# One chunk of an input load cut into transfers of 112, 8 and 8 partitions, in a fused cross-covariance attention and StarReLU kernel

## The chip, the cores and the metric

The kernel runs on one core of a Trainium2 chip. The metric is the device time of one execution in microseconds. Before the change it is 718.32 us, the median of four runs (718.17 to 718.49).

## The reference

For each of 4 batches, `q`, `k` and `v` are 6080 x 256 arrays in float32. The attention is taken between the 256 channels, not between the tokens, and its result goes through a small two-layer network:

```python
qn = q / (np.linalg.norm(q, axis=1, keepdims=True) + 1e-06)    # norms over the 6080 tokens
kn = k / (np.linalg.norm(k, axis=1, keepdims=True) + 1e-06)
s = kn.transpose(0, 2, 1) @ qn / tau                           # 256 x 256 per batch
s = s - s.max(-1, keepdims=True)
a = np.exp(s); a /= a.sum(-1, keepdims=True) + 1e-09
x = (v @ a).reshape(24320, 256)
h = x @ w_in                                                   # 256 x 2048
r = np.maximum(h, 0.0)
out = (s_moe * (r * r) + b_moe) @ w_out                        # 2048 x 256
```

## The kernel before

**Start.** Nothing of the network can run until the channel matrix of batch 0 is known, and that needs every row of `q` and `k` of batch 0: 6080 rows of 256 floats each, 12.5 MB in all. The rows are cut into 13 chunks (`make_chunks`): eleven of 512 rows (128 partitions, four rows in each), one of 256 rows (128 partitions, two rows each) and one of 192 rows (96 partitions, two rows each). Below, k4 is the `k` part of chunk 4, the fifth chunk, q4 its `q` part, and so on.

Chunks 0 and 1 are loaded as float32 by the queues of SyncE and ScalarE and cast on VectorE and ScalarE. All later ones are loaded by GpSimd's queue, which turns float32 into float16 on the way. `Gram.load` (line 118) issues one transfer for the `k` part and one for the `q` part of a chunk (line 132): 512 KB read and 256 KB written for a chunk of 512 rows. GpSimd's program order is k2, q2, k3, q3, ... k9, q9, then k10, k11, k12, q10, q11, q12, then the first tile of `v`, five pieces of `w_in`, a second tile of `v`, four pieces of `w_out`, and so on.

Eight semaphores are used in turn by GpSimd's transfers. A transfer has to wait until the one eight places ahead of it, which has the same semaphore, has landed. So at most eight of GpSimd's transfers are in flight. A chunk's tile comes from `qk_pool`, which has eight buffers; chunk 12 takes the buffer of chunk 4.

**Use of a chunk.** For each chunk TensorE adds `q`-transposed times `k` into the 256 x 256 matrix `s_ps` (`Gram.mm`, line 148). ScalarE and VectorE square both arrays, and VectorE folds the squares (`norm_ops`, lines 171 to 221), for the norms. `keep_busy` (line 477) puts idle matmuls after chunks 5 to 9. After the last chunk come the norms (lines 244 and 248), their inverse (line 269), the exponential (line 300), and the product of the channel matrix with `w_in` into `wa` (lines 327 and 343).

**The rest.** From then on TensorE works through 48 groups of 512 tokens: `h` from `wa` and the transposed `v` (line 658), and the second layer (lines 730 and 826). The Gram matrices of batches 1 to 3 are computed between these steps; their chunks are loaded by the same function. The order on every engine is the program's.

Of the kernel before, what the change touches and what calls it, by code (L numbers as in the profile page):

```python
# [17 lines left out]
def kernel(  # L18
# [12 lines left out]
    nc = tc.nc  # L31
    P = 128
# [23 lines left out]
    def po(ins):  # L56

        tc.keep_in_program_order(ins)
        return ins
# [51 lines left out]
    class Gram:  # L111
# [7 lines left out]
        def load(self, c, parts=(0, 1)):  # L119

            at, np_, jc = self.chunks[c]
            if 0 in parts:
                self.raw[c] = qk_pool.tile([P, 2, JC, C], FP16, tag="qk", name="qk")
            t = self.raw[c]
            direct = self.b == 0 and c < NDIRECT
            for i in parts:
                src = (k, q)[i]
                rows = src[self.b, at : at + np_ * jc, :].rearrange("(p j) c -> p j c", j=jc)
                if direct:
                    (nc.sync, nc.scalar)[i].dma_start(out=raw32[:, c, i], in_=rows)  # L130
                else:
                    po(nc.gpsimd.dma_start(out=t[:np_, i, :jc, :], in_=rows))
            self.tiles[c] = t[:, 1], t[:, 0]

        def cast(self, c):
# [437 lines left out]
    for i, f in enumerate(folds):  # L573
        early.setdefault(FOLDS[i], []).append(f)
    at_step(14, lambda: po(nc.vector.tensor_scalar_mul(
        out=s_out, in0=s_bc, scalar1=1.0 / (LAM * LAM))))
# [343 lines left out]
```

## Time and profile before

| | |
|---|---|
| median of four runs | 718.32 us |
| the profiled execution | 718.25 us, of which the span from the first to the last instruction is 716.5 us and 1.75 us lie around it |
| mean granted TensorE clock | 0.997 |
| TensorE busy (matmul) | 697.0 us, 97% |
| VectorE, ScalarE, GpSimd busy | 624.2, 545.0 and 111.1 us |
| GpSimd's transfers (q0) | 43.40 MB, 38.1% of the 16 DMA engines' span |
| read from and written to HBM | 78.91 MB and 24.90 MB |

All times in the views are microseconds from the start of the span. In the chain of waits, each line has a start, a length, and what the end of the kernel was waiting for in that time. In a timeline, the bracket at the end of a line has the idle time of the engine ahead of the instruction and what ended it. A transfer is shown on the engine that issues it, with the time for the issue; its landing is later.

### The profile page before, as it was taken

What the parts mean: (1) busy time and instruction counts of PE and PEld (TensorE: products, weight loads), DVE (VectorE), ACT (ScalarE), POOL (GpSimd) and SP (SyncE); (2) the same over time, 40 slices, a digit from 0 to 9 for tenths busy, and PEclk for the clock granted to TensorE, in tenths of its full rate; (3) what the DMA queues carried; (4) which work ended last, traced back from release to release, by engine and by line L of the source; (5) the groups of instructions that cost most, each with busy time, mean ns of one, the idle gap of its engine ahead of it and who ended that gap; (6) DMA issues with size and microseconds to landing.
All of it is one profiled execution on the core that took longest, in us unless ns stands there. A gap on an engine that the chain in (4) does not pass through costs nothing.

```text
span 716.5 us, 17491 instructions
## 1 busy us (share of the span) xinstructions
PE 697.0 (97%) x7421; PEld 503.6 (70%) x7421; DVE 624.2 (87%) x877; ACT 545.0 (76%) x592; POOL 111.1 (16%) x189
## 2 busy tenths in 40 slices
PE   4699999999999999999999999999999999999998
PEld 2456777776677777777677777777668777777777
DVE  4889999988789989998889899998887888888886
ACT  5779877787777777778777778777877777777875
POOL 4532332102101222111010222110000000000000
PEclk9999999999999999999999999999999999999999
DMA  9999999636565978444663877853323333321202
GB/s 235 207 258 167 167 175 135 121 90 121 111 126 108 136 134 144 112 89 94 137 146 54 148 133 125 153 91 76 100 63 75 94 71 75 97 60 46 82 31 75
DMA packets 87454, 83.47 MB, mean 116 GB/s; under 512 B 56304, under 2 KB 62256, under 8 KB 87376
## 3 DMA queue, kind: packets, MB, share of 16 engines
q0 software_dynamic: 26608, 43.40, 38.1%
q1 hardware_dynamic: 60192, 37.64, 21.7%
q8 instruction: 58, 0.95, 0.6%
q10 hardware_dynamic: 576, 1.31, 0.5%
q14 instruction: 20, 0.16, 0.1%
HBM read 78.91 MB, written 24.90 MB: 145 GB/s over the span
## 4 chain that ended last, share of the span: by engine, by line
PE 93%; DMA 3%; DVE 2%; ACT 2%; issue 0%; ACTq 0%; DVEq 0%
PE h_ps L658 45%; PE o_ps L826 40%; PE s_ps L148 4%; PE wa_ps L327 2%; DMA qk<-in_k_dram 1%; DMA raw<-in_q_dram 1%; ACT sq L177 1%; PE o_ps L730 1%; DVE f L191 1%; PE o_ps L704 0%; ACT r L668 0%; ACT r L269 0%; DVE sq L174 0%; PE n_ps L244 0%; DVE o_sb L686 0%
## 5 line engine op out<-in xcount | busy, mean ns | idle before, releaser
L668 ACT ACTIVATE r<-h_ps 128x1024 f16<-128x1024 f32 (+1 forms) x384 | 388.7, 1014 | 151.6 <-PE h_ps L658 146.9
L658 PE MATMUL h_ps<-vT,wa 128*128 128x512 f16 (+7 forms) x1632 | 452.2, 364 | 0.6 <-ACT wa L320 0.5
L826 PEld LDWEIGHTS <-S 128*128 128x128 f16 x2944 | 198.0, 98 | 84.8 <-issue 0.4
L826 PEld LDWEIGHTS <-g 128*128 128x128 f16 x2208 | 155.0, 98 | 74.1
L681 DVE TENSOR_TENSOR g<-r 128x2048 f16<-128x2048 f16 (+2 forms) x150 | 174.8, 1165 | 14.0 <-ACT r L668 13.4
L826 PE MATMUL o_ps<-T,S 128*128 128x128 f16 x2208 | 183.3, 219 | 0.1
L658 PEld LDWEIGHTS <-wa 128*128 128x128 f16 x1632 | 135.8, 98 | 20.6 <-ACT wa L320 0.8
L826 PE MATMUL o_ps<-w_out,g 128*128 128x128 f16 x1472 | 134.2, 219 | 0.2 <-DVE u L686 0.2
L686 DVE SCALAR_TENSOR_TENSOR o_sb<-o_ps,s_out,u 128x256 f32<-128x256 f32 x138 | 66.5, 482 | 50.8 <-PE o_ps L826 48.8
L679 ACT ACTIVATE g<-r 128x1024 f16<-128x1024 f16 (+1 forms) x97 | 100.3, 1034 | 0.2
L148 PE MATMUL s_ps<-qk 128*128 128x256 f16 (+1 forms) x384 | 71.8, 289 | 14.3 <-ACT qk L139 9.1
L386 POOL DMA_DIRECT2D v<-in_v_dram x48 | 31.0, 650 | 263.4 <-DMA vT<-v 186.7
L686 DVE SCALAR_TENSOR_TENSOR u<-o_ps,s_out,rowconst 128x256 f32<-128x256 f32 x138 | 65.9, 478 | 0.0
L826 PE MATMUL o_ps<-w_out,S 128*128 128x128 f16 x736 | 63.5, 219 | 0.0
L826 PE MATMUL o_ps<-N,g 128*128 128x128 f16 x736 | 63.4, 219 | 0.0
L207 POOL DMA_DIRECT2D f<-f x30 | 26.3, 878 | 224.0 <-DVE f L191 192.5
L755 DVE TENSOR_TENSOR S<-S,g 128x2048 f16<-128x2048 f16 (+1 forms) x47 | 56.4, 1201 | 1.3
L177 ACT ACTIVATE sq<-qk 128x1024 f16<-128x1024 f16 (+2 forms) x53 | 54.5, 1041 | 3.9 <-DMA qk<-in_k_dram 2.3
L753 DVE TENSOR_TENSOR S<-g 128x2048 f16<-128x2048 f16 (+1 forms) x47 | 56.1, 1193 | 0.0
L759 DVE TENSOR_TENSOR S<-g,S 128x2048 f16<-128x2048 f16 x46 | 56.0, 1216 | 0.0
L757 DVE TENSOR_TENSOR S<-g 128x2048 f16<-128x2048 f16 x46 | 55.9, 1216 | 0.0
L148 PEld LDWEIGHTS <-qk 128*128 128x128 f16 (+1 forms) x384 | 33.0, 103 | 21.0 <-ACT qk L139 9.6
(83 smaller groups left out, 314.3 us busy)
## 6 DMA issues: line engine op xcount, KB each, us to landing
out_dram<-o_sb SPq DMA_DIRECT2D x42, 512.0 KB, 2.9
v<-in_v_dram POOLq DMA_DIRECT2D x47, 256.0 KB, 5.0
qk<-in_k_dram POOLq DMA_DIRECT2D x42, 256.0 KB, 6.8
qk<-in_q_dram POOLq DMA_DIRECT2D x42, 256.0 KB, 7.5
f<-f POOLq DMA_DIRECT2D x30, 128.0 KB, 3.2
vT<-v SPq DMA_TRANSPOSE x182, 3.0
out_dram<-o_sb SPq DMA_DIRECT2D x10, 256.0 KB, 4.7
w<-in_moe_w_out_dram POOLq DMA_DIRECT2D x4, 512.0 KB, 10.1
```

The source lines that it names most:

```text
L148: po(nc.tensor.matmul(self.s_ps[:, ch, :], qc[:np_, j, ts(ch, P)], kc[:np_, j, :], start=(c == 0 and j == 0 and ch == 0), stop=(c == len(s ...
L177: po(nc.scalar.activation(out=st["sq"][:np_, a, js, :], in_=(qc, kc)[a][:np_, js, :], func=AF.Square))
L658: po(nc.tensor.matmul(dst, wa[:, ci, ts(m, P)], src, start=(ci == 0), stop=(ci == CH - 1), skip_group_check=True))
L668: po(nc.scalar.activation(out=r16[:, :, i % 2, :n], in_=h_tiles.pop((g, i))[:, :, :n], func=AF.Relu))
L679: po(nc.scalar.activation(out=dst, in_=src, func=AF.Square))
L681: po(nc.vector.tensor_mul(dst, src, src))
L686: po(nc.vector.scalar_tensor_tensor(out=dst, in0=src, scalar=s_out, op0=ALU.mult, in1=add, op1=ALU.add))
L753: po(nc.vector.tensor_add(T[1], A21, A22))
L755: po(nc.vector.tensor_sub(T[2], T[1], A11))
L757: po(nc.vector.tensor_sub(T[3], A11, A21))
L759: po(nc.vector.tensor_sub(T[4], A12, T[2]))
L826: po(nc.tensor.matmul(st[name][:, j, :], a()[:, i, ts(j, P)], w[:, i, :], start=first, stop=last, skip_group_check=True))
```

## The change

In batch 0, the two transfers of chunk 4 become six. Each of k4 and q4 is loaded by three transfers, of partitions 0 to 111, 112 to 119 and 120 to 127. The bytes, their places and everything else in the program stay.

```diff
@@ -129,7 +129,9 @@
                 if direct:
                     (nc.sync, nc.scalar)[i].dma_start(out=raw32[:, c, i], in_=rows)
                 else:
-                    po(nc.gpsimd.dma_start(out=t[:np_, i, :jc, :], in_=rows))
+                    cuts = (0, 112, 120, P) if self.b == 0 and c == 4 else (0, np_)
+                    for p0, p1 in zip(cuts, cuts[1:]):
+                        po(nc.gpsimd.dma_start(out=t[p0:p1, i, :jc, :], in_=rows[p0:p1]))
             self.tiles[c] = t[:, 1], t[:, 0]
```

## The prediction

> **What bounds the kernel now.** I read the page first, for the engines and the DMA over the span.
>
> ```profile
> PE 697.0 (97%) x7421; PEld 503.6 (70%) x7421; DVE 624.2 (87%) x877; ACT 545.0 (76%) x592; POOL 111.1 (16%) x189
> PE   4699999999999999999999999999999999999998
> DMA  9999999636565978444663877853323333321202
> ```
>
> TensorE is full in every slice but the first two (17.9 us each), where DMA is full. The change lies there. Next, the chain of waits in order of time, cut to the first 80 us:
>
> ```profile
> 1.20 8.70 DMA raw<-in_q_dram
> ...
> 20.47 9.46 DMA qk<-in_k_dram
> 29.93 0.02 issue
> 29.96 1.07 ACT sq L177
> ...
> 37.28 0.60 PE h_ps L658 x2
> ```
>
> Up to 30 us the end waits for loads of `q` and `k`. What TensorE waits for after that, from the waits between 37 and 130 us, and there is no line at all after 130 us:
>
> ```profile
> PE h_ps L658 <- ACT wa L320: 0.5, 1, 0.5
> PE o_ps L826 <- DVE u L686: 0.2, 1, 0.2
> ```
>
> So from 37 us on 0.7 us is all the slack there is: whatever the start gains or loses goes through to the end, one for one. Now GpSimd's timeline, which issues the loads:
>
> ```profile
> 5.23 0.60 POOL L132 DMA_DIRECT2D qk<-in_q_dram  x1
> 10.35 0.54 POOL L132 DMA_DIRECT2D qk<-in_k_dram  x1 [4.53 <-DMA qk<-in_k_dram]
> 11.38 0.53 POOL L132 DMA_DIRECT2D qk<-in_q_dram  x1 [0.50 <-DMA qk<-in_q_dram]
> 12.63 0.53 POOL L132 DMA_DIRECT2D qk<-in_k_dram  x1 [0.72 <-DMA qk<-in_k_dram]
> 13.95 0.53 POOL L132 DMA_DIRECT2D qk<-in_q_dram  x1 [0.79 <-DMA qk<-in_q_dram]
> ...
> 20.47 0.53 POOL L132 DMA_DIRECT2D qk<-in_k_dram  x1 [0.98 <-ACT sq L177]
> ```
>
> Eight are issued by 5.8 us (the last is q5); then k6 waits until k2 has landed, q6 for q2, and so on, one issue per landing. The issue itself (0.53) is less than half of the 1.25 between landings: GpSimd is not the limit. The answer for line 132 agrees, and gives the price of a wait instruction:
>
> ```profile
> L132 POOL DMA_DIRECT2D qk<-in_k_dram x11: 522/530/675, 1.4 to 23.0; - x11
> L132 POOLq EVENT_SEMAPHORE  x8: 17/43/43, 13.9 to 22.4; - x8
> DMA to landing us min/median/max: 7.0/9.6/13.4
> ```
>
> The 9.6 us to landing is eight transfers of 1.25 us queued one behind the other. The trace also records, for each transfer, one completion per DMA engine, and each packet. In the loaded stretch an engine takes one row of 4 KB (2 KB written) every 0.154 us and 0.02 us for a completion: 8 x 0.154 + 0.02 = 1.25 us, the pitch of the landings. The engines form two groups that keep their distance: nine complete a transfer some 0.6 us ahead of the other seven (q4: first engine at 15.35, last at 16.11). A landing is that of the slowest engine. So the start is 16 engines working through rows without a gap, and the number of rows on the slowest engine is what can change.
>
> **The change, part by part.**
>
> *Rows per engine.* The bytes stay. 112 partitions over 16 engines are 7 rows each. The other 16 rows of k4, and of q4, go in two transfers of 8. Spread over all 16 engines in turn, they make it 8 rows again: 0. If both transfers of 8 go to the same eight engines, these have 9 + 9 rows for k4 and q4 and the others 7 + 7: 2 x 0.154 = 0.31 us more or less. Where the eight are of the early nine, the late seven gain 0.31 and the eight, 0.6 ahead, lose 0.31 unnoticed: -0.31 us. Where the late ones get them: +0.31. No transfer of under 96 partitions and full rows is in this trace, so which engines take 8 rows isn't shown. The nearest rows are k12 and q12 (96 partitions): they land 0.53 and 0.50 us after the one ahead of them, k11 and q11 (128 partitions, same row size) 0.61 and 0.65, so a smaller number of partitions is spread evenly. I take 0, and keep -0.31 and +0.31.
>
> *Completions.* Four more transfers, each with a completion on every engine: 4 x 0.02 = +0.08 us in full on the path. The upper bound is a fixed price per transfer that shows only for small ones. The half-size k11 lands 0.61 after k10, against 1.25 / 2 = 0.63: no fixed part to be seen when others are queued. A rule of the Trainium skill speaks against the change: the page "DMA: Bandwidth & Descriptors", sections "Anatomy of one DMA" and "Rules for kernel authors", gives a transfer a fixed part of about 2.0 us, says that under 64 KB one pays mostly overhead (these are 32 KB), and advises against cutting by partitions. By that, paid in series, the sum would be 4 x 2.0 = 8 us more (726 us); the landings at 0.61 us and at 1.25 us here are closer together than that fixed part, so with a full queue it overlaps.
>
> *GpSimd's queue.* Four more issues, 4 x 0.53 = 2.1 us of an engine that idles between issues. But the eight places now hold less. By 5.8 us k2, q2, k3, q3, three parts of k4 and the first of q4 are issued. The other parts of q4 wait for k2 and q2 (10.35, 11.38), k5 for k3 (12.63, was 4.71), q5 for q3 (13.95, was 5.23), k6 for the first part of k4 (about 15.0, was 10.35). From k6 on every transfer again waits for the same one as before, and by k9 (17.92) the old times are met. What hides this is the queue: when k5 is issued at 12.63, q3, k4 and q4 are still to be served, until 15.35 on the first engine and 16.11 on the last: a cover of 2.7 us. Where the trace shows a load issued into an empty queue (the load of `v` at 59.1 us), its first packet starts 1.24 us after the issue. So k5 is there at 13.9, 1.5 us early; q5 at 15.2, for 16.6; k6 at 16.2, for 17.8. Cost 0. The far bound is the first load, k2: issued at 1.44, its first packet starts at 5.6, 4.2 us later. By that k5 comes at 16.8 and the engines stand still for 0.7 (late ones) to 1.5 us (early ones). I take 0, by the row in the same state (a queue in use).
>
> *Waits.* The users of chunk 4 now wait for three semaphores in place of one. At 17 to 43 ns a piece that is two more on TensorE, one each on ScalarE and VectorE. TensorE idles ahead of each chunk (1.5 us at 18.72), ScalarE's square of k4 and VectorE's of q4 would be late by 0.04 and have the next chunk's arrival as cover: 0; uncovered, 0.1 us. Nothing is queued behind the waits on GpSimd but the loads told of.
>
> *Instruction fetch.* TensorE's code comes over a DMA engine, 16 KB at a time; one such packet at 35.30 took 0.97 us, and the second piece of `w_in` finished 1.4 us later on one engine than on the other fifteen. Two more instructions move that fetch by some 0.1 us. Taken as 0; between -0.4 and +1.0 where it meets another transfer.
>
> Sum against the profiled execution: 718.25 + 0.08 = 718.33. The median is 0.07 above that execution, so 718.4 us, and no measurement of this kernel tells 0.08 us from nothing: about 0.2%, 1.4 us, is what it can tell.
>
> **The rivals.**
>
> 1. *Same eight engines.* The two transfers of 8 go to the same half of the engines. For: nothing says that the next one starts where the last ended. Price -0.31 + 0.08 = -0.23 (718.1) or +0.39 (718.7). Both are within 0.2%. The skill's same page ("Why a DMA increments its semaphore by 16 and not by 1") says that a transfer takes the largest divisor up to 16 of its partitions as its number of engines, 8 here, from a cursor that goes round; by that the sum is +0.08, and no run here shows it.
>
> 2. *One engine (slower).* A transfer of 8 partitions is given whole to one engine, and all four to the same one. That engine has 2 x 7 + 4 x 8 = 46 rows in place of 16: 30 x 0.154 = 4.6 us, which every later landing inherits as the queue is never empty: 723.0. With four different engines it is 6 rows, 0.9 us: 719.3, within 0.2%. It decides from 10 extra rows on one engine (1.5 us). Against it: the even spread of 96 partitions. For it: no transfer as small is in the trace.
>
> 3. *A hole in the queue.* k5 takes 4.2 us to its first packet: +0.7 to +1.5, 719.1 to 719.9. Against: 1.24 us in the later loads.
>
> 4. *The clock.* Windows between 19.5 and 36.5 us:
>
> ```profile
> 19.50:22.80 3.30, 1.78 (x13) 1.08 (x10) 3.06 (x7) 2.32 (x3) 1.06 (x2) 1.00 1.12 209
> 22.90:26.20 3.30, 1.30 (x10) 0.92 (x11) 3.09 (x7) 2.73 (x3) 1.59 (x3) 1.00 1.12 209
> 26.30:29.60 3.30, 3.30 (x15) 2.08 (x14) 2.79 (x6) 1.94 (x2) 1.67 (x3) 0.50 1.13 206
> 33.10:36.50 3.40, 3.06 (x45) 2.14 (x44) 2.06 (x5) 3.00 (x9) 2.70 (x5) 1.00 1.28 200
> ```
>
> After a stretch with 1.30 us of matmuls the clock (0.50, third from the right) was half for one stretch, under cover of the loads. Were it half between 33.1 and 36.5, where matmuls are on the path, half of 3.06 is lost: +1.5 us, 719.9. The chunks would have to move by far more than 0.1 us against the stretches.
>
> **How the numbers follow.** Forecast 0.42; same eight 0.25; one engine 0.12 for the same one, 0.05 for four; hole 0.08; clock 0.04; 0.04 for a gain over 0.2% by something not seen, as no row holds 1.4 us to be gained. Slower by over 0.2% is one engine 0.12 and the upper ends of hole and clock, 0.02 each: 0.16. Faster: 0.04. Within: 0.80. The range: from 718.1 less the runs' 0.2 below, 717.9, to 719.6, which takes in four engines and most of the hole, and leaves out about 0.2.
>
> **What would show it.** Right: GpSimd's issues at 10.35 and 11.38 are the small parts of q4, k5 at 12.6, q5 at 14.0; k10 lands within 0.4 us of 29.93; line 658 starts at 37.3 to 37.4. Rival 1: the gap of 0.6 us between the engines' groups closes or widens by 0.6. Rival 2: one engine's completions trail from k4 on. Rival 3: DMA share falls at 15 to 17 us. Wrong altogether: line 658 moves by over 1.4 us, or the time after it does.

## The result, and the profile after

The changed kernel takes 719.39 us (median of 41 runs, 718.37 to 720.60) against 718.30 us (61 runs): a ratio of 1.0015, with a 95% interval of 1.0010 to 1.0019. It is slower by 1.1 us, inside the range and inside 0.2%, but clear of zero and not the 0.1 us of the forecast. The profiled execution took 719.54 us with a span of 717.8 us, 1.3 us longer than before. Lines of the code stand two lower in the changed kernel: 658 is 660 there.

The page of the changed kernel, busy times and the two rows of slices that were read before:

```profile
PE 698.2 (97%) x7421; PEld 504.3 (70%) x7421; DVE 624.2 (87%) x877; ACT 545.1 (76%) x592; POOL 113.3 (16%) x193
PE   4799999999999999999999999999999999999998
DMA  9999999646465978444672877843323333321202
```

The work is the same; GpSimd has four more issues (2.2 us). The chain of waits of the changed kernel, in order of time:

```profile
17.65 8.75 DMA qk<-in_q_dram
...
26.69 8.12 DMA qk<-in_q_dram
34.81 0.02 issue
34.83 0.43 DVE sq L176
...
38.59 0.60 PE h_ps L660 x2
```

Line 660 starts at 38.59, line 658 started at 37.28: all 1.3 us are lost before that. The chain no longer ends its loads with k10 at 29.93 but with q12, at 34.81. Before the change q12 was complete at 33.44. The waits of TensorE between 37 and 130 us show nothing new behind it; the first line is the start itself, 1.3 us later:

```profile
PE r_ps L340 <- ACT eT L302: 0.5, 1, 0.5
PE h_ps L660 <- ACT wa L322: 0.5, 1, 0.5
PE o_ps L828 <- DVE u L688: 0.2, 1, 0.2
```

GpSimd's timeline has the order that was foreseen (small parts of q4 at 10.34 and 11.37, k5, q5, then k6 and the rest as a burst):

```profile
10.34 0.50 POOL L134 DMA_DIRECT2D qk<-in_q_dram  x1 [4.54 <-DMA qk<-in_k_dram]
11.37 0.50 POOL L134 DMA_DIRECT2D qk<-in_q_dram  x1 [0.53 <-DMA qk<-in_q_dram]
12.63 0.60 POOL L134 DMA_DIRECT2D qk<-in_k_dram  x1 [0.76 <-DMA qk<-in_k_dram]
13.95 0.54 POOL L134 DMA_DIRECT2D qk<-in_q_dram  x1 [0.72 <-DMA qk<-in_q_dram]
15.05 0.53 POOL L134 DMA_DIRECT2D qk<-in_k_dram  x1 [0.56 <-DMA qk<-in_k_dram]
```

What holds q12 is seen in VectorE's timeline, which squares it (`96x512`). Before the change the squares of q10, q11 and q12 follow each other without a wait:

```profile
32.31 1.57 DVE L174 TENSOR_TENSOR sq<-qk 128x1024 f16<-128x1024 f16 x3 [0.18 <-DMA qk<-in_q_dram]
```

In the changed kernel VectorE stops ahead of q12, and in the same time, between 32 and 34.5 us, the DMA queues have an entry that the loads don't explain (q0 is GpSimd's queue, q8 carries instructions):

```profile
32.59 1.06 DVE L176 TENSOR_TENSOR sq<-qk 128x1024 f16<-128x1024 f16 x2 [0.27 <-DMA qk<-in_q_dram]
34.83 0.42 DVE L176 TENSOR_TENSOR sq<-qk 96x512 f16<-96x512 f16 x1 [1.18 <-DMA qk<-in_q_dram]
```

```profile
q0 software_dynamic: 481, 0.49, 118.5%
q8 instruction: 1, 0.02, 2.4%
```

VectorE idles 1.18 us for q12. In the same stretch a packet of queue q8 runs: a piece of code, 16 KB, which took 0.974 us from 32.80 on. In the kernel before, the same stretch has no packet of q8; the first one came at 35.30, as the queues of that kernel between 34.9 and 37 us show:

```profile
q0 software_dynamic: 517, 0.41, 126.8%
q8 instruction: 1, 0.02, 2.9%
```

That q8 is TensorE's code is read from its size: the page has 58 packets and 0.95 MB, about 64 bytes for each of TensorE's 14,940 instruction records (an instruction record is one instruction in the trace), so 256 to a packet; and between two packets TensorE goes on by 254 records on average (170 to 356). The changed kernel has two instructions more on TensorE, both of them waits (97 against 95).

By the completion records, fifteen DMA engines finish q12 at 33.70 or before, and one at 34.81. So of the 1.37 us that q12 is late, 1.11 belong to one engine, and 0.26 (33.44 to 33.70) to something else.

### The profile page after: what moved, and what is told of

The parts are those of the page before. It is cut to its first block, busy times and chain, and to the rows that moved or that the text cites. A ratio compares the mean times of both kernels' runs of the same rounds, so it can differ in the third digit from the quotient of the medians.

```text
span 717.8 us, 17499 instructions
## 1 busy us (share of the span) xinstructions
PE 698.2 (97%) x7421; PEld 504.3 (70%) x7421; DVE 624.2 (87%) x877; ACT 545.1 (76%) x592; POOL 113.3 (16%) x193
## 3 DMA queue, kind: packets, MB, share of 16 engines
q10 hardware_dynamic: 576, 1.31, 0.5%
## 4 chain that ended last, share of the span: by engine, by line
PE 93%; DMA 4%; DVE 1%; ACT 1%; issue 0%; POOL 0%; POOLq 0%; ACTq 0%
PE h_ps L660 45%; PE o_ps L828 40%; PE s_ps L150 5%; DMA qk<-in_q_dram 2%; PE wa_ps L329 2%; DMA raw<-in_q_dram 1%; PE o_ps L732 1%; PE o_ps L706 0%; ACT r L670 0%; DVE sq L176 0%; DVE o_sb L688 0%; DVE S L757 0%; DVE S L755 0%; DVE g L683 0%; DVE S L759 0%
```

## The experiments

Three theories were set against each other. **Theory 1**: TensorE's two more wait instructions move the code fetch, which then takes a DMA engine while q12 is on it. **Theory 2**: the rows of the small transfers go to the same eight engines, and a queue that holds less lets an engine run dry, so that one engine is late for good. **Theory 3**: each small transfer has its price.

In the table, "records" are TensorE's instruction records in the trace (loads of weights, matmuls and waits), "fetch" is the start of the first packet of q8, "q12" the completion on the fifteenth and on the sixteenth engine, and "h" the start of line 658 (660). These come from one profile each. The times are medians beside those of the kernel before on the same chip.

| kernel | records | fetch | q12, 15th and last | h | us | before |
|---|---|---|---|---|---|---|
| before | 14940 | 35.30 | 33.42, 33.44 | 37.28 | 718.30 | |
| changed | 14942 | 32.80 | 33.70, 34.81 | 38.59 | 719.39 | 718.30 |
| e1, cut into 112 and 16 | 14941 | 32.69 | 33.37, 34.78 | 38.55 | 719.43 | 718.17 |
| e2, no cut, one idle matmul more | 14942 | 32.57 | 33.62, 34.75 | 38.52 | 719.43 | 718.17 |
| e3, changed, one idle matmul less | 14940 | 35.66 | 33.48, 33.87 | 37.70 | 718.63 | 718.17 |
| e4, changed, second profile | 14942 | 32.44 | 33.61, 34.61 | 38.56 | 719.48 | 718.17 |
| e5, no cut, one idle matmul less | 14938 | 35.25 | 33.40, 33.41 | 37.26 | 718.18 | 718.28 |
| e6, no cut, idle matmul late | 14942 | 35.22 | 33.25, 33.26 | 37.09 | 718.18 | 718.28 |
| e7, k4 and k8 cut, one idle matmul less | 14940 | 35.44 | 33.38, 33.70 | 37.53 | 718.33 | 718.28 |
| e8, as e3, second profile | 14940 | 35.03 | 33.26, 33.32 | 37.15 | 718.07 | 718.53 |
| e9, as e7, second profile | 14940 | 35.47 | 33.32, 33.61 | 37.45 | 718.41 | 718.53 |

e4, e8 and e9 are single executions; of the others e1, e2, e3, e5, e6 and e7 have 11 runs each.

**e1: 112 and 16.**

```diff
-                    cuts = (0, 112, 120, P) if self.b == 0 and c == 4 else (0, np_)
+                    cuts = (0, 112, P) if self.b == 0 and c == 4 else (0, np_)
```

> Chunk 4 of k and q cut into 112 and 16 partitions: the tail of 16 rows is one transfer and not two of 8. Theory 1 (the time is lost to TensorE's code fetch, which now meets q12 on one DMA engine, because TensorE has two more wait instructions): TensorE gets one piece less or none more, so the fetch may come at another moment; 718.3 where q12's last completion is at 33.4 to 33.6, 719.4 where one engine completes q12 over 1 us behind the other fifteen. Theory 2 (the rows of the two transfers of 8 go to the same eight engines, the engine that is left ahead runs dry while k6 is awaited, and is late for good): 16 rows are one per engine, the nine engines stay 0.6 us ahead of the seven, nothing is rebalanced; only four places of eight are left for whole transfers, one more than before, so no engine runs dry: k10 lands at 29.95 to 30.0 and the time is 718.4. Theory 3 (each small transfer has a price of its own on the path, +1.07/4 = 0.27 us): two more transfers in place of four, +0.53, 718.8.

719.43 us, ratio 1.0017 (1.0008 to 1.0026). Two more transfers in place of four cost as much as the change, where theory 3 expected 718.8. The engines kept their two groups, and the fifteenth completes q12 at 33.37, not later than before. So the transfers themselves cost nothing that is seen here. But TensorE has one wait instruction more, the fetch comes at 32.69, and one engine completes q12 at 34.78. Theory 2 expected 718.4.

**e2: no transfer touched.** The keys of `FILL` count the chunks from the end: -9 is chunk 4, -8 chunk 5. Each idle matmul is two records, a load of weights and a matmul.

```diff
-    FILL = {-8: 1, -7: 1, -6: 1, -5: 2, -4: 2}
+    FILL = {-9: 1, -8: 1, -7: 1, -6: 1, -5: 2, -4: 2}
```

> The kernel before with one idle matmul more, after chunk 4, and no transfer cut: TensorE's code is longer by the load of weights and the matmul, under cover of its wait for chunk 5. Theory 1 (the code's length moves the fetch that stood at 35.30): the fetch comes earlier, some 32.8, q12 completes about 1.1 us late on one engine and the time is 719.2 to 719.5. Theories 2 and 3 (rows and transfers): no transfer is changed, 718.3.

719.43 us, ratio 1.0019 (1.0011 to 1.0028): the whole loss of the change, without the change. The fifteenth engine completes q12 at 33.62 and the last at 34.75. VectorE's and TensorE's timelines of this run have the two lines of the changed kernel:

```profile
34.77 0.42 DVE L174 TENSOR_TENSOR sq<-qk 96x512 f16<-96x512 f16 x1 [1.15 <-DMA qk<-in_q_dram]
38.52 0.60 PE L658 MATMUL h_ps<-vT,wa 128*128 128x512 f16 x2 [0.48 <-ACT wa L320]
```

**e3: the change, with TensorE's code at its old length.**

```diff
-    FILL = {-8: 1, -7: 1, -6: 1, -5: 2, -4: 2}
+    FILL = {-7: 1, -6: 1, -5: 2, -4: 2}
```

> The changed kernel without the idle matmul after chunk 5: TensorE's code is shorter by a load of weights and a matmul, as long as before the change, and the six transfers stay. Theory 1: the fetch is back behind q12 (35 us), q12 completes at 33.7 at the latest and the time is 718.5 (0.2 to 0.3 us of the changed kernel's loss, the late engine, stay). Theories 2 and 3: 719.4 as the changed kernel. If the clock takes the missing matmul amiss, it is half in one stretch more before 33 us, under cover of the loads.

718.63 us. With all six transfers in place, the fetch is back at 35.66, VectorE squares q12 without a wait, and h starts at 37.70:

```profile
32.75 1.57 DVE L176 TENSOR_TENSOR sq<-qk 128x1024 f16<-128x1024 f16 x3 [0.20 <-DMA qk<-in_q_dram]
37.70 0.60 PE L660 MATMUL h_ps<-vT,wa 128*128 128x512 f16 x2 [0.48 <-ACT wa L322]
```

Theory 1 holds for 0.8 us (719.43 in e1 and e2, 718.63 here). What is left is 0.46 us, which is just not clear of zero (interval of the ratio 0.9999 to 1.0017); in the profile q12 is complete at 33.87, 0.43 late, on one engine 0.39 behind the next.

**e4: a second profile of the change.**

> The changed kernel once more, for a second profile. Theory 1: TensorE's fetch is again at 32 to 33.4 us and one engine completes q12 about 1.1 us behind the rest; 719.4. Theory 2: again one engine runs dry at 17.4 to 17.6 us and completes k6 some 0.3 us behind the rest. If either moment differs by more than 0.5 us from the first profile, it is chance within an execution, and only times can tell.

The fetch comes at 32.44, and the engine that it holds up is there (by q11 already, 34.46). At k6 the last engine is 0.3 us behind the middle one, but not alone: three more are beside it. The fetch is no accident of one execution; the late engine of theory 2 varies.

**e5: the control for e3.** The same removal of the idle matmul in the kernel before.

> The kernel before without the idle matmul after chunk 5, no transfer cut: the control for the changed kernel without that matmul (718.63 against 718.17 of the kernel before). Theory 1 (only the moment of the code fetch counted; in that run it was back at 35.7) with theory 2 (the 0.4 us left over are the late DMA engine): this one has neither, 718.2, q12 complete at 33.4. If taking the matmul away costs something by itself (the clock), the time is 718.4 to 718.7 and q12 is complete at 33.4 all the same.

718.18 us, ratio 0.9998 (0.9989 to 1.0007), fetch at 35.25, q12 at 33.41. Taking the idle matmul away costs nothing, so the 0.46 us of e3, if they are more than chance, belong to its transfers. The fetch holds up one engine here too, 1.35 us behind the other fifteen (before: 1.39), but in the second piece of `w_in`, which lands at 37.39, when line 658 has already started (37.26).

**e6: the same addition, behind the loads.**

```diff
     transpose_v(0)
-    keep_busy(1)
+    keep_busy(2)
     first_block()
```

> The kernel before with one idle matmul more at the end of the start, after the transposes of the first tile of v, where TensorE waits for the exponential; no transfer cut. The code is as long as with the idle matmul after chunk 4, which moved the fetch to 32.6, but the addition stands behind all the loads of q. If what counts is the place of the code that is run when the fetch is due, the fetch stays at about 35.3 and the time is 718.2 (up to 718.4 if the matmul isn't covered). If the total length of the code counts, the fetch goes to 32.6 and the time to 719.4.

718.18 us, ratio 1.0001 (0.9992 to 1.0010), with the fetch at 35.22. The code has as many records as in e2; only their place differs. So the length of the whole code doesn't decide when the fetch comes: the same addition moved it when it stood after chunk 4, and not behind the loads.

**e7: as many rows moved, two small transfers at a time.**

```diff
-                    cuts = (0, 112, 120, P) if self.b == 0 and c == 4 else (0, np_)
+                    cuts = (0, 112, 120, P) if self.b == 0 and i == 0 and c in (4, 8) else (0, np_)
```

and without the idle matmul after chunk 5.

> Only k is cut into 112, 8 and 8, in chunk 4 and in chunk 8, and the idle matmul after chunk 5 is left out, so that TensorE's code is no longer than before the change. As many rows move from the seven late engines to the early ones as in the change, but with two small transfers on the way at a time and not four. Theory 2 (the queue held too little, one engine ran dry): none runs dry, the two groups of engines end up together, q12 is complete at 33.2 (0.31 earlier for the rows, 0.08 later for the completions) and the time is 718.0, 0.2 below the kernel before. If the late engine comes from the small transfers themselves, it is there again and the time is 718.6.

718.33 us, ratio 1.0000 (0.9991 to 1.0009), and no gain: q12 at 33.70 on one engine, the other fifteen by 33.38. From 11 us to the end of these loads no packet takes over 0.18 us, so none of the slow packets that follow a dry queue in the changed kernel is there, and yet one engine is late. It falls back at k4 (16.16 at q4, the next 15.92). Theory 2 as it stood falls: the queue is not the only source of the late engine.

**e8 and e9: second profiles of e3 and e7.**

> The changed kernel without the idle matmul after chunk 5 a second time, for another profile of the one late engine (q12 complete at 33.87, the next engine at 33.48). If the late engine is made by packets that take far over 0.17 us after an engine ran ahead, such packets are in the trace again and one engine is again 0.3 us or more behind from k5 or k6 on. If it is chance, the engines are within 0.5 us of each other and q12 is complete at 33.3.

> k4 and k8 cut, a second time, for another profile of the one late engine, which was there without any long packet (q12 at 33.70, the next at 33.38). If one of the seven late engines is among the eight that get the rows of the small transfers, it falls back by 0.15 us at k4 and again at k8, against the six others that gain 0.15 each time, and the same is seen again; if it was chance, q12 is complete at 33.2.

In e8 one engine ran ahead (k5 at 16.33, the next 16.87), then had packets of 0.26 to 0.48 us, and was back in the pack at q5: q12 was complete at 33.32, earlier than before the change, in a single execution of 718.07 us. In e9 the late engine is there again, without a long packet, 0.24 us behind the next at q4 and 0.29 at q12. In the changed kernel the same eight engines take all the small transfers, but the engines that lead differ between executions (nine and seven in the profile of before, eight and eight in e5). Where one of the late ones is among the eight, it should fall back further and the start end later; where none is, the start should end earlier. The trace doesn't name the engine of a packet, but on an engine a packet starts as the one ahead ends, so the last engine can be followed. In e7 it has the rows of the small transfers: it completes the three parts of k4 at 14.25, 14.42 and 14.60, a row apart each, and those of k8 at 24.47, 24.64 and 24.82. For e8 and e9 the account fits, but is argued and not shown. No version was found that is faster than the kernel before in a timed comparison.

## Why the prediction was right or wrong

**Right.** The start passes its delay on one for one: h moved by 1.31 us and the span by 1.3. GpSimd's issues came where the working put them (10.34, 11.37, 12.63, 13.95, 15.05). Waits and completions were of no weight: e1 has two more transfers with q12's fifteenth completion at 33.37. The fixed 2.0 us of a transfer in the Trainium skill ("DMA: Bandwidth & Descriptors", "Anatomy of one DMA") did not add up in this full queue: the four transfers more would have been 8 us in series, and the kernel lost 1.1. The clock (0.52 and 0.50, third from the right) was half for two stretches in place of one, both under cover of the loads and over before 30 us:

```profile
22.90:26.20 3.30, 2.31 (x9) 1.37 (x9) 3.09 (x7) 2.94 (x3) 1.59 (x3) 0.52 1.12 209
26.30:29.60 3.30, 3.15 (x13) 2.06 (x14) 2.79 (x6) 1.77 (x2) 1.52 (x3) 0.50 1.12 207
```

It has no part in the loss: in e2 the clock is full in both stretches, and the loss is the same.

**Wrong: the term "Instruction fetch".** The working took it as 0, with +1.0 as its far end, because "two more instructions move that fetch by some 0.1 us". No row stood behind the 0.1 us. One or two records more ahead of chunk 5 move the fetch by 2.5 to 2.9 us (35.30 to between 32.44 and 32.80): it jumps. It then runs while q12, the last load that the start waits for, is on the engine, and the measured price is 1.37 us at q12, 1.11 of it on that engine alone; in time it is +1.26 us in e2, where only the idle matmul was added. The fetch had been found and priced, up to +1.0 "where it meets another transfer", but the transfer that it would meet, the one that the path ends with, was not looked for. Why it jumps is open. With 14,940 records or fewer it came late in all profiles, with one or two more ahead of the last loads it came early; TensorE had started 276 records when the fetch came at 35.30, and 197 at 32.80.

**The range held by luck.** 719.39 lies under its upper end of 719.6, but that end was set by four engines that each get one small transfer and by the hole in the queue. The term that made most of the loss had no part in it.

**Rival 1, "same eight engines", is what the rows do.** In the trace of the changed kernel, engines take 7, 1 and 1 rows of k4 and of q4, or 7 and none; none takes a whole small transfer, as rival 2 had it. After q4 the groups are gone: one engine leads, fifteen are together, and the last completes k5 at 17.26 and q5 at 18.52, 0.10 and 0.16 earlier than before. These gains are not clear of chance: q5 is complete between 18.49 (e6) and 18.83 (e2) in the four profiles in which no transfer is cut. The skill's cursor that goes round the engines (same page, "Why a DMA increments its semaphore by 16 and not by 1") would have sent the second transfer of 8 to the other half. The eight engines for eight partitions are as it says, but the going round is not seen here, and the measurement decides. The same section has an exception for some direct copies, partitions / 16, rounded up, to each engine, and that fits what is seen: one row on each of the same eight engines. The forecast of 0 for the rows rested on the even spread of 96 partitions, which says nothing about the order of two transfers of 8.

**Rival 3, the hole, came in small.** The engine that led ended its last packet of q5 at 17.42 (its completion is recorded at 17.72) and got its first packet of k6 at 17.64, 2.6 us after the issue at 15.05, where the working had 1.24 us. Then three of its packets took 0.42, 0.52 and 0.48 us in place of 0.17. 0.22 dry and 0.9 in slow packets make the 1.1 us by which this engine fell back: from 0.4 us ahead of the other fifteen, which lie within 0.4 us, to 0.3 behind them. With this engine as the last, k6 is complete 0.18 us later than before (20.09 against 19.91). At q12 it is the fifteenth, at 33.70, which is the +0.26. That this is the price of the hole is argued from one profile: in the four profiles without a cut the fifteenth completes q12 between 33.25 and 33.62.

So in this profile the 1.3 us read as a gain of 0.2 (0.16 at q5), a loss of 0.3 to 0.4 by the hole and 1.1 by the fetch, where the forecast had 0.08 of completions. The experiments show only the 1.1 (e1, e2, e3); the smaller two are of the size by which executions differ. The bound of 0.2% was too coarse as well: 41 against 61 runs tell 1.1 us from nothing.

## What to carry to other kernels

Where a start is bound by DMA, look in the trace for the code fetches of the longest program, and ask which transfer each meets: one wait instruction more on an engine can move a fetch onto the last load of the path. An edit of loads that comes out slower should be tried once with the other engines' code at its old length (here by an idle matmul less) before the loads are blamed. And a transfer is complete when the slowest of its 16 engines is: moving rows between them pays only if the late ones are known, and these changed between executions.

## What the runs showed of the hardware that was not expected

- TensorE's code came in packets of 16 KB, each on one DMA engine; the first one took 0.97 to 0.98 us in all profiles. Where it met q12 under a full load queue (changed kernel, e1, e2, e4), one engine completed q12 1.0 to 1.4 us behind the other fifteen, and all that waits for q12 waited with it.
- One instruction record more on TensorE (e1) was enough to move the first of these fetches by 2.6 us; an idle matmul after chunk 4 (e2) costs 1.26 us, the same matmul behind the loads (e6) nothing.
- Two transfers of 8 partitions, issued one after the other, went to the same eight engines, for k4 and again for q4.
- An engine that ran out of work for 0.22 us took three packets of 0.42 to 0.52 us before it was back at 0.17.
